# Opening an attention and MLP kernel by token tile: first tile on GpSimd, one PSUM bank and one copy per tile, the first two query heads in 128-token pieces

## The chip, the cores and the metric

The kernel runs on one core of one Trainium2 chip. The metric is the device time of one execution in microseconds, the median of several runs. A profiled execution is a separate run with its own time. Engine names are those of the profile: PE is the matrix engine, PEld its weight loads, DVE the vector engine, ACT the scalar engine, POOL the GpSimd engine, SP the sync engine, which here only issues transfers.

## The reference

The input x has 2048 tokens of width 576. It is normalised without learned factors, and the normalised xn goes into two branches.

```python
xn = _layernorm(x)
# A: 32 query heads, 16 key/value heads, head width 128, the last 512 cached keys only
q = (xn @ wq).reshape(B, Sq, 32, 128).transpose(0, 2, 1, 3)
k = repeat(k_cache[:, :, Sk - 512:, :], 2);  v = repeat(v_cache[:, :, Sk - 512:, :], 2)
s = (softmax(q @ k.T * 128 ** -0.5) @ v).transpose(0, 2, 1, 3).reshape(B, Sq, 4096) @ wo
# B: a small MLP with shifted channel groups, then a large one (576 -> 4608 -> 576)
h = gelu(_layernorm(xn) @ w1);  x1 = xn + shifted(h) @ w2
g = silu(x1 + gelu(_layernorm(x1) @ w3) @ w4)
return x + s * g
```

Everything is bfloat16 in memory.

## The kernel before, in words

The 2048 tokens are four blocks of 512, and a block is four tiles of 128 tokens (`TB = 4`). The width 576 is cut into five column chunks of 128, the last of 64 (`NDC = 5`). The first long stage is attention. It runs as 128 units `u`, block after block and head after head. For each unit, `stage_q` makes the queries of one head for 512 tokens (five matmuls 512 wide, or four where the remainder chunk is handled two heads at a time by `rest_q`) and copies them out of PSUM; `stage_s` makes four score matmuls 512 wide and four exponentials on ACT; `stage_v` makes sixteen matmuls 129 wide against the values and divides by the row sums on DVE; `stage_t` transposes the result by a transfer. Into the gaps of the units, lists `fill` and `pe_fill` place the other work: the output projection, the small MLP, the normalisation of the next block, and `prep_k`, which transposes the keys of one key head (four 128x128 transposes into a bank of `ps_wo`, one copy on DVE to `kT`). PE's order is written out by hand in this stage: the loop over `u` runs under `tc.manual_schedule(engines={SP, POOL, PE})`, so that SP, POOL and PE execute in the order of the program text. The second long stage is the large MLP.

What stands before unit 0 is the opening, and there the order of all five engines is written by hand. It works on block 0 as a whole:

- The tiles of x come in by transfers on the queues of SP and ACT (lines 319 to 324). SP then issues, in this order, the keys of heads 0 and 1, the keys of heads 2 and 3 (`load_k(0, nc.sync, 2)`, line 287), the query weights of heads 0 and 1 and of heads 2 and 3 (each a transfer of 512 rows, line 334, and one of the last 64 rows, line 336), the values of heads 0 and 1, the next query weights, and so on. POOL fills constant tiles (lines 327 to 343) and then issues the values of heads 2 and 3 and all later loads.
- `ln1_first` takes mean and variance of tiles 0 to 2 on DVE (lines 382, 383) and those of tile 3 on ACT (lines 386, 387), takes square roots on ACT (385 for tile 0, 389 for the others) and reciprocals on DVE (395, 397), and writes the normalised tiles: 0, 1 and 2 on DVE (line 392), 3 on ACT (line 400, with the bias from line 399).
- Meanwhile PE runs matmuls on the identity whose results nobody reads (`warm`, line 828; `warm_behind`, line 831, which waits for a statistic).
- `tr1_first` transposes the normalised tiles on PE (line 415). The outputs lie by column chunk: all four tiles of a chunk side by side, two chunks in one PSUM bank, three banks (`x_banks`). `xT_first` copies chunk by chunk, 512 wide, to `xT_b[0]`, three on DVE (line 423) and two on ACT (line 421), so that the first copy waits for the last tile.
- `keys_first` transposes the keys of heads 0 and 1, later of heads 2 and 3 (line 431); each pair goes to `kT` by one copy 1024 wide (lines 843 and 848).
- `stage_q(0)` and `stage_q(1)` make the queries of heads 0 and 1 (line 471, copies at line 481). Unit 0 follows.

The other key heads, from 4 on, are transposed in the units (`if g > 3: pe_late.append((2 * g - 3, g))`).

Of the kernel before, what the change touches and what calls it, by code (L numbers as in the profile page):

```python
# [8 lines left out]
P = 128  # L9
# [22 lines left out]
def kernel(  # L32
# [179 lines left out]
    with ExitStack() as actx:  # L212
# [70 lines left out]
        def load_k(i, eng=None, step=4):  # L283
            kst_t[i] = x1_pool.tile([P, TB, D], BF16, name="x1")
            dst = kst_t[i][:].rearrange("p a b -> p (a b)")[:, 0:4 * W].rearrange("p (g a) -> p g a", g=4)
            for g in range(0, 4, step):
                (eng or nc.gpsimd).dma_start(
                    out=dst[:, g:g + step, :],
                    in_=A_k_cache[0, 4 * i + g:4 * i + g + step, K0:, :].rearrange("g (p kc) d -> p g (kc d)", p=P))
# [40 lines left out]
        with tc.manual_schedule(engines={SP}):  # L330
            load_k(0, nc.sync, 2)
            for m0 in (0, 2 * Dh):
                cols = slice(m0, m0 + 2 * Dh)
                nc.sync.dma_start(out=wq_b[0][:, 0:NF, cols],
                                  in_=A_wq[0:NF * P, cols].rearrange("(kc p) m -> p kc m", p=P))
# [30 lines left out]
        def ln1_first():  # L366


            x, xn = x_t.pop(0), xn_b[0]
# [3 lines left out]
            nb = small.tile([P, 1], FP32, name="nr_e")  # L373
            y = small.tile([P, TB], FP32, name="nr_y")
            scrap = wo_sb[:, 0:2, :].rearrange("p a b -> p (a b)").bitcast(FP32)
            t = TB - 1
            nc.scalar.activation(out=y[:, 0:1], in_=eps_t[:], func=ACT.Sqrt)
            hw = D // 2
            for i in range(t):
                st = small.tile([P, 2, 6], FP32, name="ln_st")  # L380
                for j in range(2):
                    nc.vector.bn_stats(out=st[:, j, :], in_=x[i][:, j * hw:(j + 1) * hw])
                nc.vector.bn_aggr(out=mv[:, i, :], in_=st[:])
                if i == 0:
                    nc.scalar.activation(out=y[:, 0:1], in_=mv[:, 0:1, 1], func=ACT.Sqrt, bias=eps_t[:])
            nc.scalar.activation(out=scrap, in_=x[t], func=ACT.Copy, scale=-1.0 / (D * root), accum_out=nb[:])
            nc.scalar.activation(out=scrap, in_=x[t], func=ACT.Square, scale=1.0 / root, bias=nb[:],
                                 accum_out=mv[:, t, 1:2])
            nc.scalar.activation(out=y[:, 1:TB], in_=mv[:, 1:TB, 1], func=ACT.Sqrt, bias=eps_t[:])

            def apply(i):
                nc.vector.tensor_scalar(out=xn[:, i, 0:D], in0=x[i], scalar1=mv[:, i, 0:1], scalar2=y[:, i:i + 1],
                                        op0=ALU.subtract, op1=ALU.mult)

            nc.vector.reciprocal(out=y[:, 0:1], in_=y[:, 0:1])
            apply(0)
            nc.vector.reciprocal(out=y[:, 1:TB], in_=y[:, 1:TB])
            nm = small.tile([P, 1], FP32, name="nr_m")
            nc.vector.tensor_scalar(out=nm[:], in0=nb[:], scalar1=y[:, t:TB], scalar2=root, op0=ALU.mult, op1=ALU.mult)
            nc.scalar.activation(out=xn[:, t, 0:D], in_=x[t], func=ACT.Identity, scale=y[:, t:TB], bias=nm[:])  # L400
            for i in range(1, t):
                apply(i)
            return mv, nb
# [3 lines left out]

        def x_banks():
            pairs = [ps_sc.tile([P, 2, QB], BF16, name="ps_x", tag="sc") for _ in range(3)]
            return [pairs[kc // 2][:, kc % 2, :] for kc in range(NDC)]  # L410

        def tr1_first(pss, tts):
            for tt in tts:
                for kc, (cst, cw) in enumerate(DCH):
                    nc.tensor.transpose(out=pss[kc][:, tt * P:(tt + 1) * P], in_=xn_t[0][:, tt, cst:cst + P],
                                        identity=ident[:, :])

        def xT_first(pss):
            for kc, ps in enumerate(pss):
                if kc // 2 == 1:  # L420
                    nc.scalar.activation(out=xT_b[0][:, kc, :], in_=ps, func=ACT.Copy)
                else:
                    nc.vector.tensor_copy(out=xT_b[0][:, kc, :], in_=ps)

        def keys_first(g0, psp, tag):
            ps = psp.tile([P, 2, W], BF16, name="ps_k2", tag=tag)
            src = kst_t[0][:].rearrange("p a b -> p (a b)")
            for g in range(2):
                for kc in range(KCH):
                    c0 = (g0 + g) * W + kc * P  # L430
                    nc.tensor.transpose(out=ps[:, g, kc * P:(kc + 1) * P], in_=src[:, c0:c0 + P], identity=ident[:, :])
            return ps
# [389 lines left out]
        with tc.manual_schedule(engines={SP, POOL, PE, DVE, ACTE}):  # L822
            mv, nb = ln1_first()
            wu = ps_sc.tile([P, QB], FP32, name="warm", tag="sc")

            def warm(n):
                for _ in range(n):
                    nc.tensor.matmul(wu[:, 0:P], lhsT=ident[:, :], rhs=ident[:, :], start=True, stop=True)

            def warm_behind(ap):  # L830
                nc.tensor.matmul(wu[:, 0:1], lhsT=ident[:, :], rhs=ap.bitcast(BF16)[:, 1:2], start=True, stop=True)

            warm(40)
            for i, n in ((1, 8), (2, 4)):
                warm_behind(mv[:, i, :])
                warm(n)
            pss = x_banks()
            tr1_first(pss, range(1))
            k01 = keys_first(0, ps_wo, "wo")
            tr1_first(pss, range(1, TB))  # L840
            xT_first(pss)
            k23 = keys_first(2, ps_po, "po")
            nc.vector.tensor_copy(out=kT[:, 0:2, :], in_=k01[:, :, :])
            e = small.tile([P, 1], FP32, name="nr_e")
            nc.scalar.activation(out=e[:], in_=nb[:], func=ACT.Exp, scale=0.0)
            stage_q(0)
            stage_q(1)
            nc.vector.tensor_copy(out=kT[:, 2:4, :], in_=k23[:, :, :])
# [478 lines left out]
```

## Time and profile before

| what | value |
|---|---|
| time before, median of 3 runs | 821.91 us (821.48 to 827.05) |
| profiled execution, its own time | 821.72 us |
| its span | 819.9 us |
| PE busy | 814.7 us, 99% of the span |
| DVE, ACT, POOL busy | 466.6, 456.1 and 96.1 us |
| first score matmul of unit 0 (line 492) | starts at 11.68 us |

The timeline gives, for each merged group of instructions, the start, the time from its first start to its last end, the engine and line, and in brackets the idle time before it and who ended it. A matmul's listed duration holds its way through the array, so the starts of neighbouring matmuls, not their durations, tell how fast PE goes. The time to landing of a transfer is counted from the start of its issue. The opening is the first 1.4% of the span.

### The profile page before, as it was taken

Reading aid. Unit: us, or ns where it says so; the run is one execution under the profiler, and the core shown is the slowest. Engines: PE = TensorE matmul, PEld = TensorE weight load, DVE = VectorE, ACT = ScalarE, POOL = GpSimd, SP = SyncE. Lnnn points to the kernel's source line nnn. Section 1 sums busy time; section 2 is a strip of 40 time slices with the busy share of each in tenths; the row PEclk is TensorE's granted clock in tenths of the full one; section 3 lists DMA queues with packets and bytes.
Section 4 is the critical chain, followed back from the end, with each engine's and each line's share of the span. In section 5 each row is a group of like instructions: output and inputs, shape, how many; then the busy total and the mean of one; then the engine's idle time right before and its main releaser. Section 6 shows DMA issues by size and latency. Waiting matters only on the chain. (4 is left out here: it accounts for less than half of the span.)

```text
span 819.9 us, 19615 instructions
## 1 busy us (share of the span) xinstructions
PE 814.7 (99%) x8031; PEld 468.9 (57%) x8031; DVE 466.6 (57%) x1447; ACT 456.1 (56%) x821; POOL 96.1 (12%) x164
## 2 busy tenths in 40 slices
PE   9999999999999999999999999999999999999998
PEld 6666655655554565665465655455555555555555
DVE  6878645678884357964346774044246636655413
ACT  7888853588783368994457983033332433334621
POOL 4343223010100111110001100000000000000000
PEclk9999999999999999999999999999999999999999
DMA  8987983363492145673035554994001221130101
GB/s 208 188 194 169 198 175 81 85 128 75 104 142 63 43 91 126 136 142 56 14 85 120 108 110 102 260 325 102 2 2 45 65 72 45 42 96 15 45 15 38
DMA packets 144156, 84.29 MB, mean 103 GB/s; under 512 B 110128, under 2 KB 136944, under 8 KB 144064
## 3 DMA queue, kind: packets, MB, share of 16 engines
q1 hardware_dynamic: 133408, 53.61, 32.8%
q0 software_dynamic: 9408, 28.15, 12.5%
q8 instruction: 63, 1.03, 0.6%
q10 hardware_dynamic: 1248, 1.25, 0.4%
q14 instruction: 29, 0.24, 0.1%
HBM read 49.17 MB, written 9.29 MB: 71 GB/s over the span
## 5 line engine op out<-in xcount | busy, mean ns | idle before, releaser
L496 ACT ACTIVATE pT<-sc 128x512 bf16<-128x512 f32 x512 | 285.5, 599 | 100.0 <-PE sc L492 91.3
L492 PE MATMUL sc<-qT,kT 128*128 128x512 bf16 x512 | 172.3, 379 | 0.0
L511 PEld LDWEIGHTS <-pT 128*128 128x128 bf16 x2048 | 134.1, 98 | 54.7 <-issue 11.0
L511 PE MATMUL po<-v_sb,pT 128*128 128x129 bf16 x2048 | 158.1, 220 | 0.0
L471 PE MATMUL psq<-xT_b,wq_b 128*128 128x512 bf16 x516 | 132.2, 379 | 0.0
L956 PE MATMUL ph<-xT_b,w_s 64*128 64x512 bf16 x976 | 127.3, 376 | 0.0
L993 PE MATMUL pm<-w_s,h 64*128 64x512 bf16 x864 | 122.1, 377 | 0.0
L535 PE MATMUL pswo<-wo_sb,oT 128*128 128x512 bf16 x512 | 116.5, 379 | 0.0
L974 ACT ACTIVATE h<-ph 128x512 bf16<-128x512 f32 x67 | 39.4, 597 | 130.6 <-PE ph L956 128.4
L516 DVE TENSOR_TENSOR o<-po,ri_b 128x256 bf16<-128x256 f32 x256 | 107.8, 421 | 6.3 <-DVE ri_b L515 0.3
L993 PEld LDWEIGHTS <-h 64*128 64x128 bf16 x1728 | 70.6, 94 | 55.4
L535 PEld LDWEIGHTS <-oT 128*128 128x128 bf16 x1024 | 65.3, 98 | 56.5
L993 PE MATMUL pr<-w_s,h 64*128 64x64 bf16 x864 | 89.9, 189 | 0.0
L471 PEld LDWEIGHTS <-wq_b 128*128 128x128 bf16 x516 | 50.4, 98 | 58.4 <-issue 1.4
L956 PEld LDWEIGHTS <-w_s 64*128 64x128 bf16 x1152 | 55.8, 94 | 48.2 <-issue 0.2
L972 DVE COPY hx<-ph 128x512 f32<-128x512 f32 x55 | 38.0, 691 | 60.7 <-PE ph L956 60.7
L515 DVE RECIPROCAL ri_b<-po 128x2 f32<-128x2 f32 x256 | 42.1, 165 | 49.5 <-PE po L511 45.5
L492 PEld LDWEIGHTS <-kT 128*128 128x128 bf16 x512 | 46.8, 98 | 25.1
L479 DVE TENSOR_TENSOR qT<-psq,rq 128x512 bf16<-128x512 f32 x62 | 42.6, 688 | 27.0 <-ACT pT L496 20.4
L270 POOL DMA_DIRECT2D wq_b<-in_A_wq_dram x30 | 23.3, 775 | 289.2 <-PE sc L492 289.2
L481 DVE CAST qT<-psq 128x512 bf16<-128x512 f32 x42 | 28.9, 688 | 33.3 <-PE psq L456 29.5
L974 ACT ACTIVATE h<-hx 128x512 bf16<-128x512 f32 x55 | 34.6, 630 | 5.9 <-DVE hx L972 1.7
(158 smaller groups left out, 720.9 us busy)
## 6 DMA issues: line engine op xcount, KB each, us to landing
wq_b<-in_A_wq_dram POOLq DMA_DIRECT2D x30, 512.0 KB, 5.2
wo_sb<-in_A_wo_dram POOLq DMA_DIRECT2D x8, 576.0 KB, 5.3
w_s<-in_B_w_dram SPq DMA_DIRECT2D x9, 512.0 KB, 7.8
w_s<-in_B_w_dram SPq DMA_DIRECT2D x10, 288.0 KB, 5.4
x_dram<-x SPq DMA_DIRECT2D x4, 576.0 KB, 3.8
x<-x_dram SPq DMA_DIRECT2D x4, 576.0 KB, 4.1
w_s<-in_B_w_dram SPq DMA_DIRECT2D x4, 576.0 KB, 8.9
s_b<-s_dram SPq DMA_DIRECT2D x4, 576.0 KB, 5.8
```

The costliest lines, as they stand in the source:

```text
L471: nc.tensor.matmul(psq[:, :], lhsT=w[:, kc, hh * Dh:(hh + 1) * Dh], rhs=xT_b[qb % 2][:, kc, :], start=(kc == 0 and not (two and hh == 1)), ...
L479: behind["qT"] = nc.vector.tensor_tensor(out=qT[:, :], in0=psq[:, :], in1=rq_t.pop(u)[:, :], op=ALU.add)
L492: nc.tensor.matmul(sc[:, :], lhsT=kT[:, g, kc * P:(kc + 1) * P], rhs=qT_t[u][:, :], start=True, stop=True)
L496: behind["exp"] = nc.scalar.activation(out=pT[:, :], in_=sc[:, :], func=ACT.Exp, scale=SCALE)
L511: nc.tensor.matmul(po[:, j, :], lhsT=pTs[kc][:, tt * P:(tt + 1) * P], rhs=v_sb[:, g, kc, 0:Dh + 1], start=(kc == 0), stop=(kc == KCH - 1))
L515: nc.vector.reciprocal(out=ri, in_=po[:, :, Dh])
L516: nc.vector.tensor_tensor(out=o[:, t0:t0 + 2, :], in0=po[:, :, 0:Dh], in1=ri.unsqueeze(2).to_broadcast([P, 2, Dh]), op=ALU.mult)
L535: nc.tensor.matmul(ps, lhsT=oT_t[qb * Hq + h][:, tt, :], rhs=wo_sb[:, h, lo:hi], start=(h == 0), stop=(h == Hq - 1))
L956: nc.tensor.matmul(ps[i][:, :], lhsT=lhsT, rhs=xT[half, kc, :], start=first, stop=last, skip_group_check=True)
L972: nc.vector.tensor_copy(out=src[:, :], in_=ps[i][:, :])
L974: nc.scalar.activation(out=h3[:, :], in_=src[:, :], func=ACT.Gelu_apprx_tanh)
L993: nc.tensor.matmul(out, lhsT=h3_t[b, fc][half, tt * P:(tt + 1) * P], rhs=w4_s[fc // WS][half, fc % WS, lo:hi], start=key not in started, s ...
```

## The change

The change rewrites the opening so that it goes tile by tile, and touches nothing after it but the place where keys 2 and 3 are transposed. From unit 0 on, every engine runs the same instructions in the same order as before, with eight transposes and two copies added.

- SP issues the query weights of heads 0 and 1 first, then the keys of heads 0 and 1, the query weights of heads 2 and 3, the values of heads 0 and 1, and only then the keys of heads 2 and 3.
- Tile 0 is normalised by POOL, ahead of the loads that POOL issues. Its reciprocal now stands on DVE between the statistics of tiles 0 and 1.
- Each tile has one PSUM bank for its five transposes and one copy 640 wide: tiles 0, 2 and 3 on DVE, tile 1 on ACT. The copy of tile 0 stands on DVE ahead of the reciprocals of the other tiles. The tiles come in the order 0, 2, 1, 3.
- The queries of heads 0 and 1 are made in pieces 128 wide, five matmuls for each head and tile: forty matmuls in place of ten.
- The keys of head 0 are transposed after the queries of tile 0, those of head 1 at the end of the opening, with a copy 512 wide each. The keys of heads 2 and 3 go to `prep_k` in units 1 and 3.
- The idle matmuls are nine 512 wide and fourteen 128 wide in place of fifty-two 128 wide, with the transposes of tile 0 among them.

```diff
         with tc.manual_schedule(engines={SP}):
-            load_k(0, nc.sync, 2)
-            for m0 in (0, 2 * Dh):
+            def wq_half(m0):
                 cols = slice(m0, m0 + 2 * Dh)
                 nc.sync.dma_start(out=wq_b[0][:, 0:NF, cols],
                                   in_=A_wq[0:NF * P, cols].rearrange("(kc p) m -> p kc m", p=P))
                 nc.sync.dma_start(out=wq_b[0][0:DR, NF, cols], in_=A_wq[NF * P:D, cols])
+            wq_half(0)
+            load_k(0, nc.sync, 2, (0,))
+            wq_half(2 * Dh)
             load_v(0, nc.sync)
+            load_k(0, nc.sync, 2, (2,))
             load_wq(1, nc.sync)
...
+            def turn(i):
+                ps = ps_sc.tile([P, NDC, P], BF16, name="ps_x", tag="sc")
+                for kc, (cst, cw) in enumerate(DCH):
+                    nc.tensor.transpose(out=ps[:, kc, :], in_=xn[:, i, cst:cst + P], identity=ident[:, :])
+                return ps
...
+            def q_tile(u, i):
+                for kc in range(NDC):
+                    nc.tensor.matmul(psq[u][:, columns(i)], lhsT=wq_b[0][:, kc, u * Dh:(u + 1) * Dh],
+                                     rhs=xT[:, kc, columns(i)], start=(kc == 0), stop=(kc == NDC - 1))
+
+            def q_out(u):
+                qT_t[u] = qT_pool.tile([P, QB], BF16, name="qT")
+                nc.vector.tensor_copy(out=qT_t[u][:, :], in_=psq[u][:, :])
+
+            stats(0)
+            nc.scalar.activation(out=y[:, 0:1], in_=mv[:, 0:1, 1], func=ACT.Sqrt, bias=eps_t[:])
+            nc.vector.reciprocal(out=y[:, 0:1], in_=y[:, 0:1])
+            apply(nc.gpsimd, 0)
+            stats(1)
...
+            stats(2)
             nc.scalar.activation(out=y[:, 1:TB], in_=mv[:, 1:TB, 1], func=ACT.Sqrt, bias=eps_t[:])
+            for _ in range(9):
+                nc.tensor.matmul(wu[:, :], lhsT=ident[:, :], rhs=ident[:, :].unsqueeze(1).to_broadcast([P, QB // P, P]),
+                                 start=True, stop=True)
+            warm_behind(mv[:, 1, :])
+            t = turn(0)
+            warm(6)
+            warm_behind(mv[:, 2, :])
+            warm(8)
+            nc.vector.tensor_copy(out=xT[:, :, columns(0)], in_=t[:, :, :])
             nc.vector.reciprocal(out=y[:, 1:TB], in_=y[:, 1:TB])
+            nc.vector.tensor_scalar(out=nm[:], in0=nb[:], scalar1=y[:, z:TB], scalar2=root, op0=ALU.mult, op1=ALU.mult)
+            nc.scalar.activation(out=xn[:, z, 0:D], in_=x[z], func=ACT.Identity, scale=y[:, z:TB], bias=nm[:])
+            apply(nc.vector, 2)
+            apply(nc.vector, 1)
+            for u in range(REP):
+                q_tile(u, 0)
+            k0 = keys(0, ps_wo, "wo")
+            t = turn(2)
+            nc.vector.tensor_copy(out=xT[:, :, columns(2)], in_=t[:, :, :])
+            t = turn(1)
+            nc.scalar.activation(out=xT[:, :, columns(1)], in_=t[:, :, :], func=ACT.Copy)
+            t = turn(z)
+            nc.vector.tensor_copy(out=xT[:, :, columns(z)], in_=t[:, :, :])
...
+            nc.vector.tensor_copy(out=kT[:, 0, :], in_=k0[:, :])
+            for u, i in ((0, 2), (1, 2), (0, 1), (0, z)):
+                q_tile(u, i)
+            q_out(0)
+            for u, i in ((1, 1), (1, z)):
+                q_tile(u, i)
+            q_out(1)
+            k1 = keys(1, ps_po, "po")
+            nc.vector.tensor_copy(out=kT[:, 1, :], in_=k1[:, :])
...
-            if g > 3:
+            if g > 1:
                 pe_late.append((2 * g - 3, g))
```

More of the change, by code (lines that the diff above doesn't have):

```diff
@@ L391, in apply @@
[L391 to L399, printed above, removed]
@@ new lines, in columns, with keys @@
+            def columns(i):
+                return slice(i * P, (i + 1) * P)
+            def keys(g, psp, tag):
+                ps = psp.tile([P, W], BF16, name="ps_k2", tag=tag)
+                src = kst_t[0][:].rearrange("p a b -> p (a b)")
+                for kc in range(KCH):
+                    c0 = g * W + kc * P
+                    nc.tensor.transpose(out=ps[:, kc * P:(kc + 1) * P], in_=src[:, c0:c0 + P], identity=ident[:, :])
+                return ps
+            psq = [ps_pq.tile([P, QB], FP32, name="psq", tag="pq") for _ in range(REP)]
@@ new lines, in q_tile @@
+            def q_tile(u, i):
[5 more added lines that the diff above has]
+                nc.vector.tensor_copy(out=qT_t[u][:, :], in_=psq[u][:, :])
+            nc.scalar.activation(out=y[:, 0:1], in_=eps_t[:], func=ACT.Sqrt)
@@ L412, in tr1_first @@
[L412 to L432, printed above, removed]
         def tr1(b, tt):
@@ L822 @@
         with tc.manual_schedule(engines={SP, POOL, PE, DVE, ACTE}):
[L823 to L848, printed above, removed]
+            first_block()
         with tc.manual_schedule(engines={SP, POOL, PE}):
```

43 lines of the change are left out of this document (23 added, 20 removed).

## The prediction

> **What bounds the kernel now.** I read the page first, to see which engine sets the time; then the timeline of the opening engine by engine, because the change lies only there; then the landings of the first transfers.
>
> ```profile
> PE 814.7 (99%) x8031; PEld 468.9 (57%) x8031; DVE 466.6 (57%) x1447; ACT 456.1 (56%) x821; POOL 96.1 (12%) x164
> ```
>
> PE's 99% is a modelled figure, so by itself it does not say that PE is the bound. The starts of PE's groups do:
>
> ```profile
> 8.02 1.03 PE L415 MATMUL ps_x<-ident,xn_b 128*128 128x128 bf16 x15
> 8.89 0.61 PE L431 MATMUL ps_k<-ident,x 128*128 128x128 bf16 x8
> 9.40 2.44 PE L471 MATMUL psq<-xT_b,wq_b 128*128 128x512 bf16 x10
> 11.68 1.03 PE L492 MATMUL sc<-qT,kT 128*128 128x512 bf16 x4
> 12.54 1.24 PE L471 MATMUL psq<-xT_b,wq_b 128*128 128x512 bf16 x5
> 13.62 0.59 PE L492 MATMUL sc<-qT,kT 128*128 128x512 bf16 x2
> 14.05 0.62 PE L511 MATMUL po<-v_sb,pT 128*128 128x129 bf16 x8
> 14.51 0.38 PE L492 MATMUL sc<-qT,kT 128*128 128x512 bf16 x1
> 14.72 0.62 PE L511 MATMUL po<-v_sb,pT 128*128 128x129 bf16 x8
> 15.18 0.59 PE L492 MATMUL sc<-qT,kT 128*128 128x512 bf16 x2
> 15.61 1.24 PE L471 MATMUL psq<-xT_b,wq_b 128*128 128x512 bf16 x5
> 16.69 0.38 PE L492 MATMUL sc<-qT,kT 128*128 128x512 bf16 x1
> ```
>
> From start to start, four matmuls 512 wide take 12.54 - 11.68 = 0.86, so 0.215 us each; eight 129 wide take 0.46, so 0.058 each; fifteen 128 wide 0.87, so 0.058 each. Between 11.68 and 16.69 lie 19 of 512 and 16 of 129: 19 x 0.215 + 16 x 0.058 = 5.01 us, and 16.69 - 11.68 = 5.01. PE runs without a hole from the first score matmul on. So two rules hold for every edit here: what moves the first score matmul earlier counts fully, and what is added to PE behind 11.68 costs fully. Ahead of it, the ten query matmuls take 10 x 0.215 = 2.15 of the 2.28 us between 9.40 and 11.68: only 0.13 us is lost there. What the old opening wastes lies before 9.40, where PE waits for the copies of x.
>
> **The change, part by part.** The new path runs along statistics, reciprocals, normalised tiles, transposes, copies, query pieces, copy of the queries, first score matmul. I follow it by these rows:
>
> ```profile
> 6.53 0.21 DVE L383 BATCH_NORM_AGGREGATE ln_mv<-ln_st 128x2 f32<-128x12 f32 x1
> 6.65 0.11 DVE L395 RECIPROCAL nr_y<-nr_y 128x1 f32<-128x1 f32 x1
> 6.80 0.43 DVE L392 TENSOR_SCALAR xn_b<-hb,ln_mv,nr_y 128x576 bf16<-128x576 bf16 x1
> 7.16 0.18 DVE L397 RECIPROCAL nr_y<-nr_y 128x3 f32<-128x3 f32 x1
> 7.37 0.21 DVE L399 TENSOR_SCALAR nr_m<-nr_e,nr_y 128x1 f32<-128x1 f32 x1
> 7.50 0.76 DVE L392 TENSOR_SCALAR xn_b<-hb,ln_mv,nr_y 128x576 bf16<-128x576 bf16 x2
> 8.92 1.09 DVE L423 COPY xT_b<-ps_x 128x512 bf16<-128x512 bf16 x3 [0.66 <-PE ps_x L415]
> 9.93 0.68 DVE L843 COPY kT<-ps_k 128x1024 bf16<-128x1024 bf16 x1
> 10.80 0.69 DVE L481 CAST qT<-psq 128x512 bf16<-128x512 f32 x1 [0.19 <-PE psq L471]
> ```
> ```profile
> 4.28 0.29 ACT L385 ACTIVATE nr_y<-ln_mv,eps_t 128x1 f32<-128x1 f32 x1 [0.87 <-DVE ln_mv L383]
> ```
> ```profile
> 7.62 0.87 ACT L400 ACTIVATE xn_b<-hb,nr_m,nr_y 128x576 bf16<-128x576 bf16 x1 [0.49 <-DVE nr_m L399]
> 9.03 1.09 ACT L421 ACTIVATE xT_b<-ps_x 128x512 bf16<-128x512 bf16 x2 [0.55 <-PE ps_x L415]
> ```
> ```profile
> 1.47 0.28 POOL masks.py:199 TENSOR_SCALAR_AFFINE_SELECT ident<-ident 128x128 bf16<-128x128 bf16 x1
> 1.71 0.30 POOL L327 MEMSET xnn_b<- 128x256 bf16 x1
> ```
> ```profile
> 4.16 0.57 POOL L343 MEMSET w_sb<- 64x576 bf16 x1
> ```
> ```profile
> 4.75 0.82 DVE L382 BATCH_NORM_STATS2 ln_st<-hb 128x6 f32<-128x288 bf16 x2 [0.57 <-DMA hb<-in_A_x_dram]
> ```
>
> *Tile 0 on POOL.* The square root ends at 4.57, the reciprocal (0.11) at about 4.76. On DVE it stands ahead of the statistics of tile 1, which wait for their transfer until 4.75 anyway: it costs nothing, and 0.1 if that tile came sooner. POOL's fillings end at 4.73, so the tile starts at about 4.85. The trace has no such operation on POOL. Lower bound: a filling of 576 columns, 0.57. Upper: the select, which reads and writes at 0.28 us for 128 columns, so at most 576/128 x 0.28 = 1.26. It reads a tensor as the select does, but without its address pattern; I take 0.9, which ends at 5.75. PE waits for the statistic of tile 1 until about 6.0, so POOL has 1.1 us before it delays the transposes; the upper bound costs 0.15. POOL's loads of values stand behind it and go out 0.6 to 1.3 us later; head 4, the first that they could be late for after heads 2 and 3, is read many units on, and heads 2 and 3 come from SP's queue.
>
> The GPSIMD Engine Reference of the Trainium skill (3.1, elementwise) puts a two-input operation at 2.6 cycles an element and says to leave elementwise work to the vector engine: as an estimate from that page, 576 columns would take 1.25 us, near my upper bound, and the sum would grow by 0.15; its 4.1 has operations with one tensor input near line rate, which the tile's would be. No row here has it.
>
> *Copy of tile 0.* The statistics of tile 2 end at 6.74. The transposes of tile 0 begin at 6.0 and are done before, so its copy starts at about 6.85. Its 640 columns lie between the rows of 512 (0.365 each) and of 1024 (0.68); on the line between them 0.45. It ends at 7.30. The reciprocals of the other tiles, which started at 7.16, now start at 7.25, and tiles 2, 1 (DVE) and 3 (ACT) end at 8.0, 8.4 and 8.6: 0.1 later than before.
>
> *Query pieces and keys.* PE's idle work ends at about 7.5, then come ten pieces (0.58) until 8.1, four transposes of head 0's keys until 8.33, and tile 2 until 8.62. Tiles 1 and 3 follow at 8.62 and 8.91, until 9.20. From a transpose's start to the copy's start is 0.32 us (the eleventh transpose of the 15, 8.60, to 8.92). So the copies are: tile 2 on DVE 8.87 to 9.32, tile 1 on ACT 9.15 to 9.80 (0.545 each for 512 columns, about 0.65 for 640), tile 3 on DVE 9.45 to 9.90. PE takes them 0.1 us after their ends: 9.42 for tile 2, ten pieces until 10.0; 9.9 for tile 1, so five until 10.28; five of tile 3 until 10.57. The copy of head 0's queries starts 0.28 later, at about 10.8, and ends at 11.49. That is where it starts and ends now. The first score matmul no longer stands behind head 1's queries, which are done by 11.2 and head 1's keys by 11.4: it starts at about 11.55 instead of 11.68. **Gain 0.13 us.**
>
> *Forty narrow pieces for ten wide ones:* 40 x 0.058 = 2.32 against 2.15, but ten of them run before 8.1 and all lie ahead of the wait for the query copy; nothing on the path.
>
> *Keys of heads 2 and 3.* Their eight transposes run now at 8.89, in the wait before 9.40, and cost nothing. They move behind 11.68, into units 1 and 3, where PE has no hole: 8 x 0.058 = 0.46. **Loss 0.46 us.** Their two copies (0.365 each) fall into DVE's waits there.
>
> *Order of the loads.*
>
> ```profile
> 2.38 0.95 SPq L287 DMA_DIRECT2D x<-in_A_k_cache_dram  x2
> 3.36 0.50 SPq L334 DMA_DIRECT2D wq_b<-in_A_wq_dram  x1
> ```
> ```profile
> x<-in_A_k_cache_dram SPq DMA_DIRECT2D x1, 256.0 KB, 4.8
> ```
> ```profile
> x<-in_A_k_cache_dram SPq DMA_DIRECT2D x1, 256.0 KB, 5.1
> ```
> ```profile
> wq_b<-in_A_wq_dram SPq DMA_DIRECT2D x1, 256.0 KB, 5.5
> ```
>
> The first three big transfers land at 2.38 + 4.8 = 7.2, at about 2.86 + 5.1 = 7.95 and at 3.36 + 5.5 = 8.9. Now the first is the weights, needed at 7.5; the keys of heads 0 and 1 come second with a small transfer ahead of them, needed at 8.1 and placed on PE ahead of tile 2. By the bytes ahead they land at about 8.05; by time from issue (3.45 + 5.1) at 8.55, which would hold up PE, and everything behind, by 0.45. I take the first, since POOL's 256 KB of values now start later. Keys 2 and 3 land by about 12.5 and are read after 14.
>
> **Sum:** 821.72 - 0.13 + 0.46 = 822.05 against the profiled execution; its time stands 0.19 below the median of the runs, 821.91. I say 822.1.
>
> **The rivals.**
>
> *A, the opening gains and the moved keys are free.* If PE waited in units 1 and 3, the eight transposes would fill holes: 821.72 - 0.13 = 821.6, and 821.3 if the copies and POOL also lie at their lower bounds. For it: ACT's exponentials are dense there. Against it: the start times above leave no hole in unit 1, and the sum to 5.01 is exact.
>
> *B, slower: PE does not reach its full rate in time.*
>
> ```profile
> 1.81 4.45 PE L828 MATMUL warm<-ident 128*128 128x128 bf16 x40 [1.81 <-POOL ident masks.py:199]
> ```
> ```profile
> L828 PEld LDWEIGHTS <-ident 128*128 128x128 bf16 x11 | 1.2, 151 | 0.0
> ```
> ```profile
> L828 PEld LDWEIGHTS <-ident 128*128 128x128 bf16 x6 | 0.4, 97 | 0.0
> ```
>
> The second row is from the window 4 to 5, the third from 6.7 to 7.2: weight loads take 151 ns, later 97, and matmuls 128 wide start 0.106 apart (40 by 6.05), later 0.058. PE sped up near 6.5, after some 4.7 us of unbroken idle work. Nine matmuls 512 wide at that slow rate, 9 x 0.424, end at 5.63; then PE waits for statistics and for POOL. If that break puts the speed-up off by as much again as the work took, say to 9.9, then 8 idle matmuls, the pieces of tile 0 and the keys cost 0.05 more each: the pieces start at 8.1 and end at 9.2, tile 2 is turned by 10.0, its copy ends at 10.75, the query copy runs from 12.2 to 12.9, the first score matmul starts at 12.95: 1.27 later, with the keys 1.73, so 823.5. It decides from the point where the row of weight loads still shows 151 ns after 7.5. Against it: the break is some 0.3 us in 4.
>
> The Trainium skill's page TensorE: Matmul & The Clock Gate (Part 1) says that the array leaves half rate after one busy window of about 3.4 us whose phase is not tied to the kernel, and (Part 4) that transposes do not count as busy; the trace agrees with the two rates. By it, the new opening has 3.8 us of counting work in place of 5, which is what raises B's chance above a few per cent.
>
> *C, a late landing or a slow POOL:* the keys at 8.55 cost 0.45, POOL at twice my upper bound 0.7; the time is 822.5 to 822.8.
>
> **How the numbers follow.** My forecast has 0.55, A 0.2, C 0.13, B 0.1; 0.02 is left. One per cent, about what a measurement of this kernel can tell from no change, is 8.2 us; no case comes near it, since the whole opening lasts 11.7. So within 1% has 0.97, and slower 0.02, faster 0.01 for what I do not see. The range reaches from A at its lower bounds, 821.3 less the 0.4 by which the two nearest runs differ, to B: 820.9 to 823.5.
>
> **What would show it.** Right: the first score matmul near 11.55, four key transposes each in units 1 and 3 with PE's starts still adding up, POOL's tile from 4.85 lasting 0.6 to 1.3, the query pieces from 7.5. Wrong: weight loads at 151 ns after 7.5; PE waiting for keys ahead of tile 2; or a first score matmul before 11.1, which means that I have overpriced the copies, and that the change gains.

## The result and the profile after

The changed kernel takes 826.49 us in the median of 22 runs (822.84 to 838.67), the kernel before 821.79 us in as many runs beside it. The ratio is 1.0053, with an interval of 1.0033 to 1.0072: half a per cent slower, where 0.04% was forecast, and outside the forecast's range. The median says little here, because the times fall into groups: of 32 runs (22 and the 10 of a later repetition) 8 lie at 822.8 to 823.1, 6 at 824.4 to 824.8, 2 at 826.3 to 826.7 and 16 at 828.6 or more. The profiled execution took 831.13 us, its span is 829.5, so it shows the last group. One of the 22, 838.67, had a lower mean granted clock (0.992, the others 0.995 to 1.0) and is left out of the ratio.

The timeline of the opening, after:

```profile
5.08 2.30 POOL L400 TENSOR_SCALAR xn_b<-hb,ln_mv,nr_y 128x576 bf16<-128x576 bf16 x1 [0.33 <-DVE nr_y L434]
7.43 0.71 PE L406 MATMUL ps_x<-ident,xn_b 128*128 128x128 bf16 x5 [1.36 <-POOL xn_b L400]
7.94 0.85 PE L388 MATMUL warm<-ident 128*128 128x128 bf16 x6
8.19 0.49 DVE L450 COPY xT_b<-ps_x 128x640 bf16<-128x640 bf16 x1 [1.41 <-PE ps_x L406]
8.65 1.01 PE L388 MATMUL warm<-ident 128*128 128x128 bf16 x8
9.46 1.27 PE L424 MATMUL psq<-xT_b,wq_b 128*128 128x128 bf16 x10
10.53 0.63 PE L417 MATMUL ps_k<-ident,x 128*128 128x128 bf16 x4
10.95 1.15 PE L406 MATMUL ps_x<-ident,xn_b 128*128 128x128 bf16 x15
12.12 1.84 PE L424 MATMUL psq<-xT_b,wq_b 128*128 128x128 bf16 x30
13.80 0.39 PE L417 MATMUL ps_k<-ident,x 128*128 128x128 bf16 x4
14.18 1.02 PE L538 MATMUL sc<-qT,kT 128*128 128x512 bf16 x4
```

POOL needs 2.30 us for tile 0. PE stands still for 1.36 us until the tile is there, and when it goes on it is slow: ten query pieces from 9.46 to 10.53 are 0.107 each, thirty pieces from 12.12 to 13.80 are 0.056 each. In the record of the granted clock that the trace holds, the full rate begins at 11.24; before it was 6.60. The first score matmul starts at 14.18 instead of 11.68. That is **2.50 us**.

From there on I compared the starts of all 512 exponentials with those of before. The shift is 2.50 in unit 0, 2.72 in unit 2, 2.95 from unit 4 on: another **0.45**, from the keys that moved into units 1 and 3. Then it stays at 2.95 to unit 57, and at the first head of the third block it jumps to 9.7. The waits of PE, from its list of waits, and the place in the timeline:

```profile
PE psq L517 <- DMA xT_b<-xn_b: 5.0, 1, 5.0
PE warm L443 <- POOL ident masks.py:199: 1.8, 1, 1.8
PE ps_x L406 <- POOL xn_b L400: 1.4, 1, 1.4
```
```profile
237.51 0.81 PE L538 MATMUL sc<-qT,kT 128*128 128x512 bf16 x3
243.35 1.86 PE L517 MATMUL psq<-xT_b,wq_b 128*128 128x512 bf16 x4 [5.02 <-DMA xT_b<-xn_b]
245.15 0.61 PE L502 MATMUL psq<-xT_b,wq_b 64*128 64x512 bf16 x2
```

The same place before, where PE has no wait:

```profile
234.47 0.81 PE L492 MATMUL sc<-qT,kT 128*128 128x512 bf16 x3
235.11 1.03 PE L471 MATMUL psq<-xT_b,wq_b 128*128 128x512 bf16 x4
```

The third block's first query matmuls wait **5.02 us** for the transfers that turn its normalised tiles, and then run at half rate: 1.86 instead of 1.03 for four. In the windows view (stretch, length, busy time and count of PE, weight loads, DVE, ACT, POOL, then the granted clock, DMA share and GB/s) the next 3 us have a clock of 0.56:

```profile
243.00:246.00 3.00, 2.65 (x8) 0.57 (x8) 0.14 (x1) 0.00 (x0) 0.00 (x0) 0.56 0.55 83
```

So the 9.7 us are 2.50 + 0.45 + 5.02, another 0.3 just ahead of the wait (0.1 of it shows in the exponentials of unit 61; at 225.52 DVE stands 0.36 ahead of a sum for the queries, and does not before), and some 1.4 for the half rate. Here are the transfers in question in SP's timeline, before and after; SP issues them in pairs, with attention results (oT) between:

```profile
219.49 5.89 SPq L524 DMA_TRANSPOSE oT<-o  x3
225.69 2.52 SPq L406 DMA_TRANSPOSE xT_b<-xn_b  x2
228.31 1.64 SPq L524 DMA_TRANSPOSE oT<-o  x1
230.00 2.59 SPq L406 DMA_TRANSPOSE xT_b<-xn_b  x2
```
```profile
222.44 6.24 SPq L570 DMA_TRANSPOSE oT<-o  x3
228.98 4.77 SPq L478 DMA_TRANSPOSE xT_b<-xn_b  x2
233.85 1.21 SPq L570 DMA_TRANSPOSE oT<-o  x1
235.11 2.59 SPq L478 DMA_TRANSPOSE xT_b<-xn_b  x2
```
```profile
DMA to landing us min/median/max: 2.6/3.7/5.4
```
```profile
DMA to landing us min/median/max: 2.6/3.8/6.8
```

The first pair takes 4.77 to issue instead of 2.52 (3.44 of it for the first transfer), the second pair starts 5.11 later than before in a schedule that is 2.95 to 3.3 late, and its last transfer, issued at about 236.5, lands 6.8 us later, at 243.3. Before, it was issued at 231.36 and landed 2.60 later, at 233.96, and PE read its block from 235.11 on: the margin was just over one microsecond.

One thing stands beside every landing of 6 us and more of that last transfer: POOL's loads of the next query weights (512 KB and twice 32 KB). After, then before:

```profile
236.64 0.79 POOL L270 DMA_DIRECT2D wq_b<-in_A_wq_dram  x1 [9.31 <-PE sc L538]
```
```profile
233.59 0.78 POOL L270 DMA_DIRECT2D wq_b<-in_A_wq_dram  x1 [9.21 <-PE sc L492]
```

After, they are issued 0.16 us behind the last transfer, before 2.23 us behind it. In the transfers' view of the changed kernel from 239 to 241, POOL's queue has 66.3% of the DMA engines' time and the queue with the transposing transfers 8.2%. In the three profiles that have the long wait (this one, its repetition and the one with block 2 normalised earlier) these loads and the last transfer are issued within 0.2 us of each other, and the transfer lands after 6.2 to 6.8. In ten others, the kernel before among them, the loads come at least 1.5 us behind and it lands after 2.6. In the three versions at the end that transpose keys by transfers it took 4.1 to 4.2 with the loads 2.5 us or more behind, so the loads are not the only thing that lengthens it. No run moves the loads alone.

### The profile page after: what moved, and what is told of

Same layout as the page of the kernel before. It is cut to its first block, busy times and chain, and to the rows that moved or that the text cites. A ratio compares the mean times of both kernels' runs of the same rounds, so it can differ in the third digit from the quotient of the medians.

```text
span 829.5 us, 19617 instructions
## 1 busy us (share of the span) xinstructions
PE 818.0 (99%) x8032; PEld 470.4 (57%) x8032; DVE 467.3 (56%) x1448; ACT 456.0 (55%) x820; POOL 98.8 (12%) x165
## 3 DMA queue, kind: packets, MB, share of 16 engines
q8 instruction: 63, 1.03, 0.5%
q10 hardware_dynamic: 1248, 1.25, 0.4%
## 5 line engine op out<-in xcount | busy, mean ns | idle before, releaser
L507 ACT ACTIVATE rq<-sc 128x512 f32<-128x512 f32 x62 | 33.6, 595 | 13.8 <-PE sc L502 13.8
```

## The experiments

All runs stand in this table: the profiled execution's first exponential (12.09 in the kernel before) and the start of PE's full rate in the clock record (6.60 before), then all times.

| run | first exponential | full rate from | median us (lowest to highest), runs | ratio to before, interval |
|---|---|---|---|---|
| e1_after_again | 14.22 | 10.50 | 828.83 (823.00 to 833.23), 10 | 1.0068 [1.0040, 1.0095] |
| e2_tile0_dve | 11.95 | 5.39 | 821.88 (821.72 to 823.38), 10 | 1.0005 [0.9995, 1.0016] |
| e3_keys_back | 12.89 | 4.88 | 823.75 (822.85 to 824.80), 10 | 1.0024 [1.0012, 1.0035] |
| e4_idle_fill | 12.76 | 6.64 | 822.94 (822.83 to 823.04), 10 | 1.0003 [0.9986, 1.0019] |
| e5_pool_alone | 12.54 | 6.68 | 821.93 (821.84 to 827.90), 10 | 1.0004 [0.9984, 1.0024] |
| e6_delay_alone | 14.71 | 5.77 | 824.27 (824.01 to 824.52), 6 | 1.0026 [1.0012, 1.0040] |
| e7_tr_earlier | 12.94 | 5.78 | 827.05 (826.38 to 829.59), 4 | 1.0062 [1.0045, 1.0079] |
| e9_four_at_once | 14.36 | 10.78 | 823.23 (823.08 to 824.78), 10 | 1.0014 [1.0000, 1.0028] |
| e10_half_tile | 13.94 | 11.01 | 822.04 (821.69 to 823.96), 10 | 0.9995 [0.9979, 1.0012] |
| e11_warm_delay | 13.93 | 6.11 | 824.02 (823.92 to 824.82), 10 | 1.0019 [1.0005, 1.0033] |
| e12_pause_alone | 14.55 | 13.04 | 823.49 (822.99 to 824.51), 10 | 1.0017 [1.0008, 1.0027] |
| f1_keys_by_transfer | 12.40 | 6.37 | 825.25 (823.54 to 826.47), 7 | 1.0037 [1.0025, 1.0049] |
| f2_keys_early | 12.40 | 5.88 | 821.29 (819.69 to 828.28), 10 | 0.9995 [0.9972, 1.0018] |
| f3_before_keys | 11.90 | 4.46 | 820.40 (819.99 to 847.52), 10 | 0.9993 [0.9970, 1.0016] |

The kernel before, run beside these, had medians of 821.60 to 821.73. Some of its own runs lie at 822.8 to 826.3, and they widen the intervals; so the groups of times are read together with the ratios. No profile shows what makes these runs of the kernel before longer.

**The changed kernel again.** No edit.

> The changed kernel once more, for a second profile. Theory: three losses add up. Tile 0 on POOL lasts about 2.3 us again and ends after 7.3; PE, which pauses for it, stays at its slow rate until about 11; the first score matmul starts near 14.2, so the opening costs 2.5, and 0.46 more for the moved keys. The fourth term comes and goes: if the transfer that turns the last tile of block 2 lands late, PE waits up to 5 us at the start of the third block, and the time is near 829; if not, near 824. Rival: the long wait at the third block is a property of the changed kernel, there in every profile; then every time is near 829 and none near 823.

POOL's row is 2.29, the pause 1.36, the full rate comes at 10.50, the wait at the third block is 4.85. The ten times are 823.0, then 824.4, 824.5 and 824.8, then six at 828.7 or more. So both late losses come and go, as the theory had it; the rival is out.

**Tile 0 on DVE.**

```diff
-            apply(nc.gpsimd, 0)
+            apply(nc.vector, 0)
```

> The changed kernel with tile 0 normalised on DVE at the same place of the program, ahead of the statistics of tile 1. Theory, POOL's 2.3 us is what broke the opening: the normalising takes 0.43 and delays the later statistics by as much; PE has no pause above 0.5 us before the transposes, reaches its full rate near 6.6 as in the kernel before, and the first score matmul starts near 12.0 instead of 14.18; steady shift against before 0.7 to 0.9, time 822.4 to 822.7. Rival, the idle work itself (nine wide matmuls and a few narrow ones) is too little to bring PE to its full rate: PE stays slow until about 11 and the first score matmul starts at 13 or later; time above 823.5.

```profile
4.76 0.43 DVE L400 TENSOR_SCALAR xn_b<-hb,ln_mv,nr_y 128x576 bf16<-128x576 bf16 x1
6.24 0.44 PE L406 MATMUL ps_x<-ident,xn_b 128*128 128x128 bf16 x5
7.61 0.72 PE L424 MATMUL psq<-xT_b,wq_b 128*128 128x128 bf16 x10
11.54 0.81 PE L538 MATMUL sc<-qT,kT 128*128 128x512 bf16 x3
```

Better than expected: the first score matmul starts at 11.54, the shift of the exponentials is -0.15 in unit 0, 0.08 in unit 2, 0.30 from unit 4 to the end, and the median is 0.2 above before. Taking POOL out takes all of the loss but the keys' 0.45. Three of ten times lie 0.8 to 1.5 higher; a late full rate would explain them, but none of the three has a profile.

**Keys of heads 2 and 3 back in the opening.**

```diff
             t = turn(z)
+            k23 = ps_po.tile([P, 2, W], BF16, name="ps_k4", tag="po")
+            ...
             q_out(1)
+            nc.vector.tensor_copy(out=kT[:, 2:4, :], in_=k23[:, :, :])
...
-            if g > 1:
+            if g > 3:
```

> The changed kernel with the keys of heads 2 and 3 loaded and transposed in the opening again, after the transposes of tile 3, with one copy for both. Theory: PE has no hole from the first score matmul on, so the eight moved transposes cost 8 x 0.058 = 0.46 there; here that loss goes, and the shift against before is the same at the first exponential and at unit 4 (about 2.5 at both, or 0.1 to 0.4 more at the first if the eight transposes fill no wait at PE's slow rate). Rival: the growth of the shift from 2.50 to 2.95 over the first four units has another cause and stays.

```profile
13.67 0.39 PE L545 MATMUL sc<-qT,kT 128*128 128x512 bf16 x1 [0.39 <-DVE kT L480]
```

The growth in units 1 to 4 is gone: the shift is 0.79 at the first exponential, 1.36 in unit 1, and about 1.36 to the end. The step in unit 1 is my own edit: the fourth score matmul takes its PSUM buffer from the same two as the new keys and waits for their copy. So this run shows where the 0.45 comes from, but gains nothing. Five times lie at 822.9 to 823.0, five at 824.5 to 824.8, and none above.

**Idle work while POOL is busy.**

```diff
             warm_behind(mv[:, 1, :])
+            warm(14)
             t = turn(0)
```

> The changed kernel with 14 more idle matmuls 128 wide between the statistic of tile 1 and the transposes of tile 0, so that PE works on while POOL normalises tile 0. POOL's 2.3 us stay. Theory: PE's pause of 1.4 us ahead of the transposes is why it stayed at its slow rate until 11.24; without the pause it changes rate near 6.6 as in the kernel before, and the first score matmul starts near 12.7: 1.0 later than before instead of 2.5, and 1.5 with the keys, time near 823.2. Rival: the change of rate does not hang on the pause but comes when it comes; then it stays slow until about 11 and the first score matmul starts at 14.2 or a little later.

```profile
5.03 2.30 POOL L400 TENSOR_SCALAR xn_b<-hb,ln_mv,nr_y 128x576 bf16<-128x576 bf16 x1 [0.29 <-DVE nr_y L434]
5.88 1.29 PE L388 MATMUL warm<-ident 128*128 128x128 bf16 x14
7.38 0.45 PE L406 MATMUL ps_x<-ident,xn_b 128*128 128x128 bf16 x5 [0.21 <-POOL xn_b L400]
8.48 0.72 PE L424 MATMUL psq<-xT_b,wq_b 128*128 128x128 bf16 x10
```

POOL is as slow as before, the transposes start as late, but the ten pieces behind them take 0.72 instead of 1.27, and all ten times lie within 822.83 to 823.04. The first score matmul comes at 12.34, 0.66 after before. This separates the two losses of the opening: POOL's work itself 0.66, the slow rate 1.84.

**Tile 0 on POOL in the old opening.**

```diff
+                    nc.vector.reciprocal(out=y[:, 0:1], in_=y[:, 0:1])
+                    nc.gpsimd.tensor_scalar(out=xn[:, 0, 0:D], in0=x[0], ...)
...
-            nc.vector.reciprocal(out=y[:, 0:1], in_=y[:, 0:1])
-            apply(0)
```

> The kernel before with one part of the change alone: the reciprocal of tile 0 stands on DVE ahead of the statistics of tile 1, and POOL normalises tile 0 from there on. The rest of the opening is the old one. Theory: POOL starts near 5.0 and takes 2.3 again, so it ends near 7.3; here the transposes stood behind idle matmuls until 8.02 anyway, PE has no pause, and DVE is free 0.3 earlier; the first score matmul starts between 11.4 and 11.7 and the time is 821.4 to 821.8. So the same POOL work costs nothing where it has cover until 8.0. Rival: POOL's work slows DVE's statistics beside it, or its 2.3 us hung on something else in the changed kernel; then the row differs from 2.3, or the statistics from 0.8, and the first score matmul comes later than 11.8.

```profile
5.02 2.30 POOL L387 TENSOR_SCALAR xn_b<-hb,ln_mv,nr_y 128x576 bf16<-128x576 bf16 x1 [0.27 <-DVE nr_y L386]
7.38 0.45 PE L416 MATMUL ps_x<-ident,xn_b 128*128 128x128 bf16 x5
```

POOL's 2.30 is there again and hidden: PE does not wait for it. The time was not quite free: 821.93 against 821.73, and the profile's first score matmul is 0.44 late, because there the statistics of tile 2 waited 0.18 for their transfer and the two tiles behind took 0.90 on DVE instead of 0.76. I did not find out whether POOL causes either.

**A pure delay.**

```diff
+            warm(52)
             pss = x_banks()
```

> The kernel before with nothing of the change, but 52 more idle matmuls 128 wide ahead of the transposes of tile 0: 52 x 0.058 = 3.0 us of pure delay, as much as the changed kernel's opening loses in the profile. Theory A, the long wait at the third block comes from the delay itself, which shifts the schedule against something that does not shift: then most times are near 829. Theory B, it does not come from the delay: all times are near 821.7 + 3.0 = 824.7, and the margin of the last transposes of block 2 ahead of the third block stays 1.0 us.

The shift is 2.61 and stays so to the end; all six times lie at 824.0 to 824.5. Theory A is out: being late does not by itself make PE wait at the third block.

**Block 2 normalised one unit earlier.**

```diff
-        ln1_at = (19, Hq + 24, 2 * Hq + 16)
+        ln1_at = (19, Hq + 23, 2 * Hq + 16)
```

> The changed kernel with the normalisation and the transposing transfers of block 2 one unit earlier in the program (about 5.6 us more time until the third block needs them). Nothing else. Theory: the wait of 5 us was a transfer landing 5 us late, so it goes in all executions, and with it the group of times near 829; what is left are the two groups of the opening, near 822.9 (PE at full rate in time) and 824.6 (PE slow until about 11). Rival: the wait moves to another transfer or another place; then times near 829 remain.

```profile
224.38 0.38 SPq L747 DMA_DIRECT2D x_dram<-x  x1
224.85 4.09 SPq L570 DMA_TRANSPOSE oT<-o  x2
229.04 3.62 SPq L478 DMA_TRANSPOSE xT_b<-xn_b  x2
232.76 1.21 SPq L570 DMA_TRANSPOSE oT<-o  x1
234.06 2.56 SPq L478 DMA_TRANSPOSE xT_b<-xn_b  x2
```
```profile
PE psq L517 <- DMA xT_b<-xn_b: 4.6, 1, 4.6
```

It failed, and teaches more than a success: the wait stayed, 4.6 us in the profile, and all four times are 826.4 or more, although PE had its full rate from 5.78 on. So the long wait does not need a slow opening. Ahead of the transfers SP's queue holds a store that waits for a sum on DVE. With the normalisation moved ahead of that sum, the store goes out at 224.38 (219.02 before, in a schedule 1.5 late), and everything behind it on SP is later, not earlier.

**The four transfers of block 2 together.**

```diff
-                    at(u1 + (3 + tt // 2 if b else 5 + tt), ...)
+                    at(u1 + (3 + (tt // 2 if b == 2 else 0) if b else 5 + tt), ...)
```

> The changed kernel with one edit on SP's queue: the four transposing transfers of block 2 are issued one after the other, where two were issued ahead of the attention result of one unit and two behind it. All other engines keep their order. In the run that normalises block 2 one unit earlier these transfers had come out 1.9 us later, behind a store that waits for DVE on the same queue, and the long wait was in all its times; so what counts is when the last one lands. Theory: the last transfer is issued some 3 us earlier, lands before the third block needs it, and times near 829 vanish; 822.9 and 824.6 remain. Rival: the four transfers side by side land late together, or the wait moves to the attention result that is now issued behind them; then times above 826 remain.

```profile
228.75 6.80 SPq L478 DMA_TRANSPOSE xT_b<-xn_b  x4
235.64 5.17 SPq L570 DMA_TRANSPOSE oT<-o  x4
```

The opening is the slow one here (full rate from 10.78, first exponential 14.36), the second transfer again takes long to issue (2.85), yet the last goes out at 234.3, PE has no wait there, and the shift ends at 3.07. The last transfer is issued 2.09 ahead of POOL's loads and lands after 2.59. Ten times of ten lie at 823.1 to 824.8. Against 16 of 32 at 828.6 and above this says that the last of these transfers made the group near 829. By their times only three of the ten, the profiled one among them, had the slow opening, so the sample is small; the run above, where the last transfer landed late and all four times are 826.4 or more, is the other half of the argument.

**Tile 0 in halves.**

```diff
-            apply(nc.gpsimd, 0)
+            for eng, lo, hi in ((nc.gpsimd, 0, hw), (nc.vector, hw, D)):
+                eng.tensor_scalar(out=xn[:, 0, lo:hi], in0=x[0][:, lo:hi], ...)
```

> The changed kernel with tile 0 halved: columns 0 to 287 on POOL, 288 to 575 on DVE at the same place. Prices POOL's operation at a second size. Theory: POOL's cost goes with the columns, 288 take about 1.2 us (half of 2.30 and a fixed part of 0.1 or so), DVE's half 0.27; tile 0 is ready near 6.1, when the statistic of tile 1 arrives too, PE has no pause above 0.5, comes to its full rate near 6, and the first score matmul starts at 11.9; time 822.0 to 822.5. Rival: POOL's 2.30 is mostly fixed; then half a tile takes about 2 us and PE pauses again.

```profile
5.06 1.41 POOL L436 TENSOR_SCALAR xn_b<-hb,ln_mv,nr_y 128x288 bf16<-128x288 bf16 x1 [0.32 <-POOL w_sb L348]
6.52 0.72 PE L406 MATMUL ps_x<-ident,xn_b 128*128 128x128 bf16 x5
8.55 1.27 PE L424 MATMUL psq<-xT_b,wq_b 128*128 128x128 bf16 x10
```

288 columns take 1.41 and 576 take 2.30: (2.30 - 1.41) / 288 = 3.1 ns for a column, and a fixed 0.52 if a straight line joins the two sizes. DVE's statistics run beside POOL in every one of these profiles, so what POOL takes alone is not shown. PE pauses for 0.4 only, and still this profile has the slow rate until 11.01; five of ten times are 821.7 to 821.9, one is 822.2, four are 823.4 to 824.0. So I was wrong on the pause: a long one is not needed for a late full rate.

**A later start at full rate.** `warm(46)` in place of `warm(14)` in the edit of the idle work.

> The changed kernel with 46 more idle matmuls between the statistic of tile 1 and the transposes of tile 0, 32 more than the 14 that cover POOL's work: PE has its full rate early, as with those 14, but the first score matmul comes about 1.5 later than there, near 13.9, as late as in the profile of the changed kernel. Tells what goes with the long wait at the third block. Theory A, the lateness of the whole schedule, together with what else the changed opening does: times near 829 are back. Theory B, the slow rate of PE in the opening itself, by the order in which the first loads and units then fall: all times near 822.9 + 1.5 = 824.4.

Full rate from 6.11, shift 2.63 at the end, ten times at 823.9 to 824.8: theory B. With the pure delay (2.61 at the third block) and this run (2.4 there), lateness by itself is ruled out twice as the trigger of the long wait: the repetition of the changed kernel had the wait at 2.6 to 2.7.

**A pause in the old opening.**

```diff
-            warm(40)
+            warm(32)
-            for i, n in ((1, 8), (2, 4)):
+            for i, n in ((1, 0), (2, 0)):
```

> The kernel before with nothing but a pause in PE's idle work: 32 idle matmuls in place of 40, and none behind the statistics of tiles 1 and 2 (8 and 4 before), so that PE works from 1.8 to 5.2 and then stands until about 7.3, when tile 0 is normalised. Theory: PE's full rate comes at the end of a window of 3.41 us that was busy, and the place of these windows differs from execution to execution; 3.4 us of work hold a whole window only rarely, so most executions keep the slow rate until 8 to 11, the first score matmul comes 1 to 2 us later than 11.68, and most times lie between 822.8 and 824. Rival: a pause by itself does not put the full rate off; then PE has it before 7, the first score matmul is near 11.2 to 11.7 and the times stay at 821.3 to 821.8.

```profile
1.81 3.59 PE L828 MATMUL warm<-ident 128*128 128x128 bf16 x32 [1.81 <-POOL ident masks.py:199]
7.11 0.72 PE L415 MATMUL ps_x<-ident,xn_b 128*128 128x128 bf16 x5 [0.33 <-DVE xn_b L392]
8.47 1.81 PE L415 MATMUL ps_x<-ident,xn_b 128*128 128x128 bf16 x15
```

Nothing of the change is in this kernel, and its profile, the slowest of the ten, loses about as much in the opening (first exponential 2.46 late): fifteen transposes take 1.81 instead of 1.03, the full rate comes at 13.04, and all ten times are 823.0 to 824.5. Shorter and interrupted idle work alone does it.

**Versions meant to beat both.** f1 is the changed kernel with tile 0 on DVE and the keys of heads 2 to 15 transposed by transfers:

```diff
+        def keys_by_transfer(g):
+            src = kst_t[g // 4][:].rearrange("p a b -> p (a b)")[:, (g % 4) * W:(g % 4 + 1) * W]
+            nc.sync.dma_start(out=kT[:, g, :].rearrange("p (a b) -> p a b", a=KCH), in_=src, transpose=True)
...
-                pe_late.append((2 * g - 3, g))
+                at(2 * g - 3, lambda g=g: keys_by_transfer(g))
```

> A version meant to beat both: the changed kernel with tile 0 on DVE, and the keys of heads 2 to 15 transposed by transfers on SP's queue in place of matmuls (4 transposes on PE and a copy on DVE for each head). Theory, PE has no hole in the units, so each transpose taken off it gains its 0.058: 56 x 0.058 = 3.2 us less than with tile 0 on DVE alone, about 818.7. Rival: the 14 more transposing transfers hold up those of the attention results on the same queue, PE waits for them in the output projection or the score matmuls wait for the keys, and the gain is below 1 or turns into a loss.

```profile
PE sc L542 <- DMA kT<-x: 4.6, 3, 2.1
```

The gain per head came, 0.11 a unit down to a shift of -0.97 in unit 16, and three waits of score matmuls for the keys took it back. f2 issues the same transfers earlier: `at(g - 2 if g < 8 else g - 1 if g < 12 else g + 3, ...)`.

> The version meant to beat both, mended: tile 0 on DVE, keys of heads 2 to 15 transposed by transfers on SP's queue, now issued one unit after the other from unit 0 on as soon as their loads have come, 3 to 13 units ahead of their first use in place of 3. Theory: the three waits of score matmuls for such a transfer (4.6 us in the run before) go, and the 56 transposes taken off PE gain their 3.2: about 818.7. Rival: the transfers hold up the attention results on the same queue, or a score matmul's wait takes in a later transfer of the same queue; then waits of 1 us and more stay and the time is above 821.

The waits are gone and the shift reaches -2.24 in unit 28. But the times scatter from 819.7 to 822.3 and one is 828.28. f3 has the opening of before, the early key transfers for heads 4 to 15, and the four transfers of block 2 together.

> Once more a version meant to beat both, with the opening of before left alone: the keys of heads 4 to 15 are transposed by transfers on SP's queue, early, in place of 48 matmuls in the units, and the four transposing transfers of block 2 are issued together. Theory: 48 x 0.058 = 2.8 us less on PE, and no late last transfer at the third block: 818.9 in nearly all executions. Rival: the added transfers make others late; then waits appear and times scatter above 820, as with the opening of the changed kernel.

Its profile is 2.74 ahead from unit 28 on, and ends 1.6 ahead (span 818.3): 1.1 of the gain is lost after the last matmul, where in f1, f2 and f3 alone an instruction fetch of 8 KB is the last transfer. Seven of ten times lie at 820.0 to 820.4, 1.2 or more below before's median, but three are 827 and above. The interval, 0.9970 to 1.0016, does not show it faster.

## Why the prediction was wrong, step by step

**Tile 0 on POOL: the mis-sized term.** "Lower bound: a filling of 576 columns, 0.57. Upper: the select ... at most 1.26 ... I take 0.9." It is 2.29 or 2.30 in all eight profiles of a whole tile. The select's row was not an upper bound: it is a 128-column operation without scalars per partition, and I scaled it as if nothing in it were particular to its kind. The Trainium skill's GPSIMD Engine Reference (3.1) puts a two-input operation at 2.6 cycles an element, from which I estimated 1.25 us. The measured 2.30 is above that too, so here the measurement decides.

**PE's slack.** "POOL has 1.1 us before it delays the transposes": right as a slack, and 2.30 used it up. The transposes came at 7.43 instead of 6.0, and by itself that puts the first score matmul 0.66 behind the old opening, 0.79 behind my sum (12.34 against 11.55, in the run with idle work in POOL's time). The prediction's case C, "POOL at twice my upper bound 0.7", is nearly this price.

**PE's rate: rival B, at 0.1, is what happened in both profiles of the changed kernel, and worse.** Its point of decision was right: slow after 7.5. Against it stood "the break is some 0.3 us in 4", which rested on POOL's 0.9. The size was wrong too: B's 12.95 stands 1.40 behind my 11.55, and the slow rate cost 1.84 (14.18 against 12.34), since the full rate came at 11.24, not 9.9. The run with a pause alone shows the mechanism without POOL, the half tile that even a 0.4 us interruption can suffice: its profile is slow, and four of its ten times lie with that profile's. What ties it together is in the clock records: the full-rate stretches last 812.37, 815.78, 808.96, 235.52 or 232.11 us, and all are whole multiples of 3.413 (238, 239, 237, 69 and 68), while their starts scatter from 4.46 to 6.68, or lie at 10.50 to 13.04. So in these traces the rate changes only at the edges of such windows, and where the edges fall differs from execution to execution. The Trainium skill's page TensorE: Matmul & The Clock Gate (Part 1) has such a window: free-running, 3413 ns, and full rate after a busy one. By it, the old opening, which keeps PE at work from 1.81 on, holds a busy window wherever the edges fall; the changed one, with 3.8 us of work and then gaps, does so only when an edge lies well. The groups 822.9 and 824.6 agree with it, and so do two profiles with the same idle work and a pause as long: with the keys back and with block 2 normalised earlier the full rate began at 4.88 and 5.78, ahead of the pause. The window need not be busy from end to end: in the last version (f3) PE's first matmul starts at 1.81 and the full rate begins at 4.46, only 2.65 us later.

**Copies, pieces, order of the loads: right.** Without POOL's tile, the changed opening starts its first score matmul at 11.54; predicted was 11.55. No matmul waited for weights or keys. POOL's first loads (the values of heads 4 and 5; those of heads 2 and 3 come from SP, not from POOL as the description of the kernel before has it) went out at 7.34 instead of 4.68, and no matmul waited for them. **The moved keys: right**, 0.46 predicted, 0.45 measured, and without them in the units the growth is gone, so rival A is out. The kernel that I predicted, with a cheap tile 0, exists: its median is 821.88, 0.2 above the kernel before, where my sum was 0.33 above. That the changed kernel came out slower, as forecast, is luck all the same: the moved keys explain 0.45 of the 4.7 us between the medians.

**The third block: not seen at all.** I wrote that nothing behind the opening changes but the keys, and took a uniform shift for granted. The rows that I quoted end at 16.69. A look at the landings of the transfers before would have shown one chain with a margin of 1 us. Shown is that the last transfer's landing makes the 5 us (in the profile the wait ends 0.1 us behind it; four at once: gone; a later SP queue: there again). Why that transfer took 6.8 us is argued only from its place beside POOL's loads. **Open** is why it slid beside them: one transfer of the first pair takes up to 3.45 us to issue in the changed kernel, and 1.2 before. It is not lateness alone, by two runs, and not the slow rate alone: the half tile and the pause alone had the slow rate until 11.01 and 13.04 in their profiles, and no wait at the third block.

## What to carry to other kernels

A row of another kind of operation is not an upper bound for one that the trace does not show: on an engine that is new to the work, ask what 2 and 3 times the estimate does to the path, and give that the weight. Idle work that warms a matrix engine is safe here only where it runs unbroken until useful work takes over; when a change puts a wait into it, price the whole stretch behind at the slow rate. Before calling a shift uniform, go through the transfers that a later stage needs and list their margins, and the other queues' loads that are issued near them: a chain with 1 us to spare is a risk in every edit ahead of it.

## What the runs showed of the hardware that I had not expected

POOL's subtract-and-multiply with two scalars per partition took 2.30 us for 576 columns and 1.41 for 288 in bfloat16, beside DVE's statistics, against 0.43 us for 576 columns on DVE: more than five times. A wait of 5 us brought PE back to half rate for one window, 3.41 us. A transposing transfer's issue alone took between 1.2 and 3.4 us on SP's queue, and its landing 2.6 to 6.8 us, for the same bytes; the longest landings fell together with 512 KB loads on POOL's queue.
